# Pooled attention and channel mix on one core: x's first blocks ahead of the weights, a shorter float64 conversion, an earlier second block, two exponentials ahead of squares

## The chip, the cores and the metric

The kernel runs on one core of one Trainium2 chip. The number that counts is the device time of one execution, in microseconds, from a launch to its end. The profile of one execution gives a span (first to last instruction); the execution's own time is a little longer than its span.

The engines are named as the profile names them: PE (matrix products; PEld is its weight load), DVE (vector), ACT (scalar functions), POOL (GpSimd) and SP, whose queue issues nearly all transfers here.

## What is computed

For each of B = 4 batches with N = 12608 tokens of 128 features, 32 inducing rows attend to all tokens, all tokens attend to the 32 results, and the outcome goes through an RWKV channel mix of inner width 1024.

```
def mab(q, kv):
    s = scale * (q @ kv.transpose(0, 2, 1))
    s = s - s.max(-1, keepdims=True)
    a = np.exp(s)
    a /= a.sum(-1, keepdims=True) + 1e-09
    return a @ kv
h = mab(I, x)          # I: the 32 inducing rows, for every batch
x = mab(x, h)
x_prev = np.concatenate([zeros, x[:, :-1, :]], axis=1)
xk = mu_k * x + (1.0 - mu_k) * x_prev
xr = mu_r * x + (1.0 - mu_r) * x_prev
k = np.maximum(xk @ w_k, 0.0)
v = k * k @ w_v
r = 1.0 / (1.0 + np.exp(-(xr @ w_r)))
return r * v
```

x, mu and the output are float32; the three weight matrices come as float64, so the kernel has to make float32 of them from their bit patterns.

## The kernel before

**Tiling.** A batch is six blocks of 2048 tokens and a tail of 320. A block is four groups of 512 tokens. Each group is four *units* of the channel mix; unit n does `up` (six matmuls into the two-bank tile `ps_a`), `square` (DVE takes the ReLU `k_t` at line 802, ACT squares it into the high part `kh` at line 807 and once more in full at line 808, POOL subtracts to the low part `kl` at line 810), and four steps later `down` (six matmuls into `ps_v`). There are 400 units, and the main loop runs over them by the step number n; two units' `up` stand together at even n. In steps 8, 12, 20, 24 and so on DVE makes `kh` itself (line 804).

**What else hangs on the steps.** Work beside the units is put into the loop by step: `at(n, f)` places f at the end of step n, `soon(n, f)` places it in step n ahead of that step's squares. `stage_a(b, j)` pools block j of batch b (the inducing rows' side) one batch ahead; `stage_b(b, j)` lets a block's tokens attend to the pooled rows, and spreads the result over the tiles `R` of its four groups by transfers.

**The head.** Batch 0 has nobody to run ahead of it, so `head()` pools its seven pieces in the order tail, block 0, ... block 5, indexed k = 0..6 there. For piece k: `tr` transposes x on PE and ACT copies it to `xt`; `scores` multiplies with the inducing rows; `maxi` takes the running maximum on DVE (lines 257 to 261); `expo` is on ACT (lines 272, 273); `etrans` (PE) and `ecopy` (DVE, line 285) turn the exponentials; `hmm` (PE, line 297) and `acc` (DVE, line 308) accumulate; `sums` (DVE, line 290) keeps the running sum. Between these, `place(n)` takes the next n steps off the list of weight conversions. The table `PARTS` says how many are taken where.

**A conversion** (`load_weight`, lines 85 to 135) of 128 x 512 weights takes six steps: exponent, mantissa, clamp, sign, low, power. DVE does lines 105, 109, 115, 120, 123, 127; ACT does 116 (mantissa to float) and 110 (ReLU of the exponent); POOL multiplies the parts at line 133. Five pieces are converted: two of w_k, two of w_v and a quarter-size one, w_r. `split_wv` (lines 159 to 164) then splits w_v into `wvh` and `wvl`.

**The loads.** The raw weights go to buffers `k_t` (w_r's to `oT`), blocks 0 to 3 of x to buffers `kh` and `kl` (two transfers of 512 KB per block, line 193), blocks 4 and 5 to the two `xb` buffers (eight of 256 KB, line 212), the tail to `xl`. Later batches load a block by one transfer of 1 MB into `xb` (line 207). All are issued by SP in program order.

**The end of the head and the start.** After piece 6's `etrans`, `spin(2)` runs ten matmuls on PE with no result that is used; then `weights_sum`, `hmm` and `hfin` give the pooled rows `hT`. `start()` makes the first four groups of stage B straight from x (`stage_b_first(g)`: `diff`, `expo` at line 725, `norm`, `turn` at line 744, `high` at 749, `low` at 753), partly ahead of the loop and partly in its first steps. Block 1 of batch 0 then goes through `stage_b` with `direct=True`; its exponential is at line 638.

**Next batch's blocks.** `stage_a(1, j)` transposes its block with four calls of `btr(c)` (DVE, line 344, into one of three `xs` buffers; then four transfers to `xt` at line 347). For block 0 these stand in steps 8 to 11, for block 1 in steps 15, 16, 17 and 19. The load of the block behind it is put at step t + 8, where t is the step at which the stage starts: for block 1 of batch 1 that is step 12.

Of the kernel before, what the change touches and what calls it, by code (L numbers as in the profile page):

```python
# [8 lines left out]
F32 = mybir.dt.float32  # L9
# [10 lines left out]
def kernel(  # L20
# [64 lines left out]
    def load_weight(dst, src, n, raw):  # L85
# [11 lines left out]
        def steps():  # L97
# [10 lines left out]
            def clamp():  # L108
                v.tensor_scalar(out=X.t, in0=X.t, scalar1=1151.0, scalar2=-896.0, op0=ALU.min, op1=ALU.add)
                nc.scalar.activation(out=X.t, in_=X.t, func=AF.Relu)  # L110
# [7 lines left out]
            def sign():  # L118
                X.r = st.tile([P, G], I32, name="aT")[:, :n]
                v.tensor_scalar(out=X.r, in0=hi, scalar1=-2147483648, scalar2=None, op0=ALU.bitwise_and)  # L120

# [4 lines left out]
            def power():  # L126
                v.scalar_tensor_tensor(out=X.t, in0=X.t, scalar=23, in1=X.r,
                                       op0=ALU.logical_shift_left, op1=ALU.bitwise_or)
                qv, tv = X.q, X.t.bitcast(F32)
                if len(dst.shape) == 3:  # L130
                    qv = qv.rearrange("p (c d) -> p c d", d=C)
                    tv = tv.rearrange("p (c d) -> p c d", d=C)
                nc.gpsimd.tensor_tensor(out=dst, in0=qv, in1=tv, op=ALU.mult)
            return [exponent, mantissa, clamp, sign, low, power]
# [191 lines left out]
    def stage_a(b, j, at, t):  # L326
# [151 lines left out]
        for bn, jn in order_a[k + 1:]:  # L478
            if jn < NBLK - 1:
                at(t + 8, lambda: load_x(bn, jn))  # L480
                if jn == NBLK - 2:
                    at(t + 8, lambda: load_x(bn, jt))
                break
# [119 lines left out]
    def stage_b(b, j, at, t, bank="b", direct=False, offsets=(0, 1, 1, 2, 3, 5, 5, 6, 6, 7, 9)):  # L603
# [80 lines left out]
        for n, f in zip(offsets, (scores, trans, maxi, sub, expo, total, recip, mult, back, high, low)):  # L684
            at(t + n, f)
# [196 lines left out]
    for j in order_h:  # L882
        load_x(0, j, pairs if j < 4 else None)
        if wloads:
            wloads.pop(0)()
# [12 lines left out]
    def spin(n):  # L898

        half = P // 2  # L900
        ps = pa.tile([P, 2, G], F32, name="ps_a")
        rhs = wvh.rearrange("p c d -> p (c d)")[:, :G]
        for i in range(3):
            nc.tensor.matmul(out=ps[:, i % 2, :], lhsT=wvh[:, i, :], rhs=rhs, start=True, stop=True)
        for i in range(n):
            for r in range(2):
                rows = slice(half * r, half * (r + 1))
                nc.tensor.matmul(out=ps[:, r, :], lhsT=wvh[rows, (i + r) % FC, :], rhs=rhs[rows],
                                 start=True, stop=True)
        for i in range(3):  # L910
            nc.tensor.matmul(out=ps[:, i % 2, :], lhsT=wvh[:, i, :], rhs=rhs, start=True, stop=True)


    PARTS_FIRST = 6
    PARTS = ((0, 0, 0), (3, 3, 0), (3, 3, 0), (3, 3, 0), (3, 3, 1), (1, 0, 0), (0, 0, 0))

    def head():
# [3 lines left out]
        for k in range(2):  # L921
            ab[k].tr()
        place(PARTS_FIRST)
        ab[0].scores()
        for k in range(NBLK):
# [7 lines left out]
            if k > 0:  # L933
                ab[k - 1].acc()
            if k == 0:
                constants()
            if k + 2 < NBLK:
                ab[k + 2].tr()
            place(PARTS[k][1])
# [3 lines left out]
            ab[k].etrans()  # L943
            ab[k].ecopy()
            if k < last:
                ab[k].sums()
                ab[k + 1].scores()
            place(PARTS[k][2])
        spin(2)
        weights_sum()  # L950
        ab[last].hmm()
# [14 lines left out]
    def start():  # L966
# [8 lines left out]
        plan = ((None, None, None, at, soon, soon, at), (at,) * 4 + (soon, soon, at), (at,) * 4 + (soon, soon, at))  # L975
# [15 lines left out]
    for b in range(B):  # L991
        t = b * UB + (4 if b == 0 else 0)
        for j in range(NBLK - 1):
# [6 lines left out]
            else:  # L1000
                stage_b(b, j + 1, at, 3, direct=True, offsets=(0, 1, 1, 1, 3, 4, 4, 4, 5, 6, 7))
# [75 lines left out]
```

## Time and profile before

| | us |
|---|---|
| runs, not profiled | 1123.52, 1127.31, 2022.45 |
| median of these | 1127.31 |
| the profiled execution's own time | 1123.31 |
| its span | 1121.5 |

The profile and the trace are of the execution that took 1123.31 us, of which 1121.5 us are the span and 1.8 us lie around it. A stretch is read from a view of busy time by windows, and a wait from a view in order of time: a row gives the start, the length, the engine, the line, the operation, the tiles, and in brackets how long the engine had been idle before it and what released it. A row of several instructions (x4) has the time of all of them. The mean granted clock of PE is 0.99 over the whole span.

### The profile page before, as it was taken

The page shows a single profiled execution, that of the slowest core. Times are in us where ns is not written, and L with a number is a line of the kernel's source. Part 1 is how long each engine was busy: PE and PEld are TensorE (multiplying, and loading weights), DVE is VectorE, ACT ScalarE, POOL GpSimd, SP SyncE. Part 2 cuts the span into 40 slices and gives each one's busy share as a digit, 9 for nine tenths or more (in the row PEclk, how much of TensorE's full clock was granted, in tenths as well). Part 3 has the DMA queues.
Part 4 walks back from the last instruction along what each step waited for, and adds up shares of the span by engine and source line. Part 5 has one row for each costly group of instructions (what it writes and reads, how often), then busy time and mean ns, then how long its engine had stood idle before and what let it go on. Part 6 is the DMA issues. An engine that isn't in the chain of part 4 may idle for free.

```text
span 1121.5 us, 19356 instructions
## 1 busy us (share of the span) xinstructions
PE 1077.1 (96%) x6610; PEld 736.2 (66%) x6610; DVE 913.1 (81%) x1301; ACT 962.4 (86%) x1101; POOL 948.3 (85%) x421
## 2 busy tenths in 40 slices
PE   5779899999999999999999999999999999999997
PEld 4546566666676666666766666667667666667775
DVE  5677789998678999998777899998776788888665
ACT  5486688898998988898998898999899989999995
POOL 2157599888888999888888998889889899999996
PEclk9999899999999999999999999999999999999998
DMA  9204575675327656757317646765414424453422
GB/s 274 77 1 119 115 155 135 146 175 133 60 39 164 138 133 144 169 134 158 60 29 139 156 109 154 162 157 114 86 31 94 91 48 95 87 97 71 88 38 35
DMA packets 267634, 123.61 MB, mean 110 GB/s; under 512 B 225648, under 2 KB 247056, under 8 KB 265232
## 3 DMA queue, kind: packets, MB, share of 16 engines
q1 hardware_dynamic: 267200, 122.35, 50.7%
q8 instruction: 53, 0.87, 0.3%
q14 instruction: 45, 0.37, 0.1%
q10 hardware_dynamic: 336, 0.02, 0.0%
HBM read 28.07 MB, written 25.82 MB: 48 GB/s over the span
## 4 chain that ended last, share of the span: by engine, by line
PE 84%; DVE 6%; SPq 4%; ACT 3%; issue 1%; DMA 1%; POOL 1%; DVEq 0%; ACTq 0%
PE ps_v L821 48%; PE ps_a L792 26%; PE ps_v L780 4%; DVE k_t L802 2%; PE pb_b L621 2%; PE pb_a L441 2%; PE pb_a L372 2%; DMA xb<-in_x_dram 1%; SPq L95 1%; ACT kh L807 1%; SPq L193 1%; SPq L601 1%; ACT k_t L808 1%; POOL kl L810 1%; DVE kh L804 1%
## 5 line engine op out<-in xcount | busy, mean ns | idle before, releaser
L810 POOL TENSOR_TENSOR kl<-k_t,kh 128x1024 fp32r<-128x1024 f32 (+2 forms) x400 | 936.6, 2381 | 135.9 <-ACT k_t L808 124.9
L802 DVE TENSOR_SCALAR k_t<-ps_a 128x1024 f32<-128x1024 f32 (+1 forms) x400 | 476.8, 1198 | 86.3 <-PE ps_a L792 64.4
L808 ACT ACTIVATE k_t<-k_t 128x1024 f32<-128x1024 f32 (+1 forms) x400 | 418.0, 1048 | 50.3 <-DVE kh L804 16.9
L807 ACT ACTIVATE kh<-k_t 128x1024 fp32r<-128x1024 f32 (+1 forms) x352 | 365.3, 1038 | 67.2 <-DVE k_t L802 66.7
L792 PE MATMUL ps_a<-R,W 64*128 64x512 f32 (+1 forms) x2400 | 332.1, 408 | 8.8 <-DVE k_t L802 7.0
L792 PEld LDWEIGHTS ps_a<-R,W 64*128 64x128 f32 x2400 | 209.4, 186 | 131.1 <-issue 52.4
L821 PE MATMUL ps_v<-kh,wvh 128*128 128x512 f32 (+1 forms) x800 | 272.3, 422 | 0.0
L821 PE MATMUL ps_v<-kl,wvh 128*128 128x512 f32 (+1 forms) x800 | 249.8, 393 | 1.7 <-POOL kl L810 1.2
L821 PE MATMUL ps_v<-kh,wvl 128*128 128x512 f32 (+1 forms) x800 | 249.9, 394 | 0.0
L821 PEld LDWEIGHTS ps_v<-kh,wvh 128*128 128x128 f32 x800 | 132.7, 189 | 95.2 <-issue 38.5
L821 PEld LDWEIGHTS ps_v<-kl,wvh 128*128 128x128 f32 x800 | 150.4, 189 | 37.6 <-POOL kl L810 2.2
L821 PEld LDWEIGHTS ps_v<-kh,wvl 128*128 128x128 f32 x800 | 150.3, 189 | 33.7
L826 DVE TENSOR_TENSOR oT<-ps_v,rT 128x512 f32<-128x512 f32 (+1 forms) x100 | 66.9, 669 | 25.0 <-PE ps_v L821 24.8
L780 PE MATMUL ps_v<-R,Wg 128*128 128x512 f32 (+1 forms) x200 | 64.2, 402 | 6.4 <-DVE oT L826 6.4
L837 DVE STREAM_TRANSPOSE ot<-oT 128x512 f32<-128x512 f32 x96 | 67.0, 698 | 0.0
L804 DVE SCALAR_TENSOR_TENSOR kh<-ps_a,k_t 128x1024 fp32r<-128x1024 f32 x48 | 58.8, 1225 | 1.7
L782 ACT ACTIVATE rT<-ps_v 128x512 f32<-128x512 f32 (+1 forms) x100 | 57.9, 579 | 0.3
L344 DVE STREAM_TRANSPOSE xs<-xb 128x512 f32<-128x512 f32 x72 | 49.9, 693 | 10.0 <-DMA xb<-in_x_dram 5.5
L780 PEld LDWEIGHTS ps_v<-R,Wg 128*128 128x128 f32 x200 | 37.2, 192 | 17.2 <-DVE oT L826 8.5
L782 ACT ACT_TABLE_LOAD x31 | 39.8, 1283 | 0.5
L667 DVE TENSOR_TENSOR hl<-pb_b,hl 128x512 fp32r<-128x512 f32 x23 | 15.9, 690 | 14.2 <-ACT hl L664 13.9
L621 PE MATMUL pb_b<-xt,hT 128*32 128x512 f32 x184 | 24.4, 603 | 0.6 <-DVE R L753 0.6
(217 smaller groups left out, 528.7 us busy)
## 6 DMA issues: line engine op xcount, KB each, us to landing
out_dram<-ot SPq DMA_DIRECT2D x184, 128.0 KB, 3.3
R<-R SPq DMA_DIRECT2D x88, 256.0 KB, 3.2
xb<-in_x_dram SPq DMA_DIRECT2D x18, 1024.0 KB, 5.8
xt<-xs SPq DMA_DIRECT2D x288, 64.0 KB, 2.0
R<-hl SPq DMA_DIRECT2D x96, 128.0 KB, 2.4
R<-hl SPq DMA_DIRECT2D x96, 127.8 KB, 2.4
kh<-in_x_dram SPq DMA_DIRECT2D x4, 512.0 KB, 7.9
kl<-in_x_dram SPq DMA_DIRECT2D x4, 512.0 KB, 7.5
```

The lines of the kernel that those rows point to most:

```text
L344: nc.vector.transpose(out=xs.rearrange("p (s q) -> p s q", q=M), in_=S.xb[j][:, :, M * c:M * (c + 1)])
L780: nc.tensor.matmul(out=ps[:, :w], lhsT=S.Wg, rhs=R[:, s, :w], start=(s == 0), stop=(s == 1))
L782: nc.scalar.activation(out=self.rT, in_=ps[:, :w], func=AF.Sigmoid)
L792: nc.tensor.matmul(out=ps[:, r, :w], lhsT=S.W[a][rows, u * P:(u + 1) * P], rhs=R[rows, k, :w], start=(n == 0), stop=(n == 2))
L802: nc.vector.tensor_scalar(out=k, in0=ps, scalar1=0.0, scalar2=None, op0=ALU.max)
L804: nc.vector.scalar_tensor_tensor(out=kh, in0=ps, scalar=0.0, in1=k, op0=ALU.max, op1=ALU.mult)
L807: nc.scalar.activation(out=kh, in_=k, func=AF.Square)
L808: nc.scalar.activation(out=k, in_=k, func=AF.Square)
L810: return lambda eng, a, z: eng.tensor_tensor(out=kl[:, :, a:z], in0=k[:, :, a:z], in1=kh.bitcast(F32)[:, :, a:z], op=ALU.subtract)
L821: nc.tensor.matmul(out=self.v, lhsT=wt[:, fc, :], rhs=kk[:, c, :], start=(fc == 0 and n == 0), stop=(fc == FC - 1 and n == 2))
L826: nc.vector.tensor_tensor(out=self.oT, in0=self.v, in1=self.rT, op=ALU.mult)
L837: nc.vector.transpose(out=ot[:, o:o + w], in_=self.oT)
```

## The change

Seven edits, in the order of the program:

1. `load_weight`: the step `sign` goes; `power` takes the sign bit and joins the exponent in one operation, since ACT's ReLU now scales by 2^23 and so does the shift; the order is exponent, clamp, mantissa, low, power. On ACT the ReLU thereby comes ahead of the mantissa.
2. The loads: the weights' five transfers are issued behind blocks 1, 2, 3, 4 and 5 of x, no longer behind the tail and blocks 0 to 3. They follow one another as before.
3. `head()`: the conversions start one piece later (no more `PARTS_FIRST`), in the rounds k = 1 to 5, and both `split_wv` come in round 5. `place(PARTS[k][1])` moves between `etrans` and `ecopy`. `sums` of a piece moves behind `acc` of that piece, one round later.
4. `warm(8)`: eight 128 x 128 matmuls of the identity, behind the tail's transposes.
5. `spin(3)`: three matmuls in place of ten, behind `weights_sum`.
6. `stage_a`: block 1 of batch 1 is loaded at step 2, not at step 12.
7. The exponentials of group 3 (line 725) and of block 1 (line 638) of batch 0 are put with `soon`, ahead of their step's squares.

```
             def clamp():
                 v.tensor_scalar(out=X.t, in0=X.t, scalar1=1151.0, scalar2=-896.0, op0=ALU.min, op1=ALU.add)
-                nc.scalar.activation(out=X.t, in_=X.t, func=AF.Relu)
+                nc.scalar.activation(out=X.t, in_=X.t, func=AF.Relu, scale=2.0 ** 23)
...
-            def sign():
-                X.r = st.tile([P, G], I32, name="aT")[:, :n]
-                v.tensor_scalar(out=X.r, in0=hi, scalar1=-2147483648, scalar2=None, op0=ALU.bitwise_and)
...
             def power():
-                v.scalar_tensor_tensor(out=X.t, in0=X.t, scalar=23, in1=X.r,
-                                       op0=ALU.logical_shift_left, op1=ALU.bitwise_or)
+                v.scalar_tensor_tensor(out=X.t, in0=hi, scalar=-2147483648, in1=X.t,
+                                       op0=ALU.bitwise_and, op1=ALU.bitwise_or)
...
-            return [exponent, mantissa, clamp, sign, low, power]
+            return [exponent, clamp, mantissa, low, power]
...
             if jn < NBLK - 1:
-                at(t + 8, lambda: load_x(bn, jn))
+                at(2 if (b, j) == (1, 0) else t + 8, lambda: load_x(bn, jn))
...
         for n, f in zip(offsets, (scores, trans, maxi, sub, expo, total, recip, mult, back, high, low)):
-            at(t + n, f)
+            (early if early and f is expo else at)(t + n, f)
...
         load_x(0, j, pairs if j < 4 else None)
-        if wloads:
+        if 0 < j < NBLK - 1:
             wloads.pop(0)()
...
+    def warm(n):
+
+        ps = pa.tile([P, 2, G], F32, name="ps_a")
+        for i in range(n):
+            nc.tensor.matmul(out=ps[:, i % 2, :P], lhsT=ident, rhs=ident, start=True, stop=True)
...
-    PARTS_FIRST = 6
-    PARTS = ((0, 0, 0), (3, 3, 0), (3, 3, 0), (3, 3, 0), (3, 3, 1), (1, 0, 0), (0, 0, 0))
+    PARTS = ((0, 0), (3, 2), (3, 2), (3, 2), (3, 2), (5, 2), (0, 0))
...
-        for k in range(2):
-            ab[k].tr()
-        place(PARTS_FIRST)
+        ab[0].tr()
+        warm(8)
+        ab[1].tr()
         ab[0].scores()
...
             if k > 0:
                 ab[k - 1].acc()
+                ab[k - 1].sums()
...
-            place(PARTS[k][1])
             if k == last:
                 ab[k].sums()
                 weights()
             ab[k].etrans()
+            place(PARTS[k][1])
             ab[k].ecopy()
             if k < last:
-                ab[k].sums()
                 ab[k + 1].scores()
-            place(PARTS[k][2])
-        spin(2)
         weights_sum()
+        spin(3)
         ab[last].hmm()
...
-        plan = ((None, None, None, at, soon, soon, at), (at,) * 4 + (soon, soon, at), (at,) * 4 + (soon, soon, at))
+        plan = ((None, None, None, at, soon, soon, at), (at,) * 4 + (soon, soon, at), (at, at, soon, at, soon, soon, at))
...
-                stage_b(b, j + 1, at, 3, direct=True, offsets=(0, 1, 1, 1, 3, 4, 4, 4, 5, 6, 7))
+                stage_b(b, j + 1, at, 3, direct=True, early=soon, offsets=(0, 1, 1, 1, 3, 4, 4, 4, 5, 6, 7))
```

Where the instructions stand now. In these lists a row is a line of the program, an operation, output<-inputs and a size; `x4` is four in a row. The changed program is a little shorter, so its line numbers in these rows are 4 smaller.

**SP, from its first transfer on.** The `k_t` and `oT` rows are the weights; `xl`, `kh`, `kl` and `xb` 128x4x128 are batch 0's x; `xb` 128x2048 is a block of batch 1. Before:

```order
L201 DMA xl<-in_x_dram 80x4x128
L95 DMA k_t<-in_moe_w_k_dram 128x1024
L193 DMA kh<-in_x_dram 128x8x128 x2
L95 DMA k_t<-in_moe_w_k_dram 128x1024
L193 DMA kh<-in_x_dram 128x8x128 x2
L95 DMA k_t<-in_moe_w_v_dram 128x4x256
L193 DMA kl<-in_x_dram 128x8x128 x2
L95 DMA k_t<-in_moe_w_v_dram 128x4x256
L193 DMA kl<-in_x_dram 128x8x128 x2
L95 DMA oT<-in_moe_w_r_dram 128x256
L212 DMA xb<-in_x_dram 128x4x128 x8
```

On the same engine, now:

```order
L197 DMA xl<-in_x_dram 80x4x128
L189 DMA kh<-in_x_dram 128x8x128 x4
L95 DMA k_t<-in_moe_w_k_dram 128x1024
L189 DMA kl<-in_x_dram 128x8x128 x2
L95 DMA k_t<-in_moe_w_k_dram 128x1024
L189 DMA kl<-in_x_dram 128x8x128 x2
L95 DMA k_t<-in_moe_w_v_dram 128x4x256
L208 DMA xb<-in_x_dram 128x4x128 x4
L95 DMA k_t<-in_moe_w_v_dram 128x4x256
L208 DMA xb<-in_x_dram 128x4x128 x4
L95 DMA oT<-in_moe_w_r_dram 128x256
```

Blocks 0 and 1 (`kh`) have no piece of the weights ahead of them now, where one and two stood; block 2 has one and block 3 two, where three and four stood; block 4 has three and block 5 four, where all five stood. w_r's small piece is behind them all.

**SP, the next rows**, up to the first spread of stage B's result (`R`). Before:

```order
L207 DMA xb<-in_x_dram 128x2048
L347 DMA xt<-xs 32x512 x16
L588 DMA R<-R 32x2x1 x2
L601 DMA R<-hl 32x1024
L601 DMA R<-hl 32x2x511
L601 DMA R<-hl 32x1024
L601 DMA R<-hl 32x2x511
L207 DMA xb<-in_x_dram 128x2048
L588 DMA R<-hl 32x2x1 x2
```

On the same engine, now:

```order
L203 DMA xb<-in_x_dram 128x2048 x2
L343 DMA xt<-xs 32x512 x16
L584 DMA R<-R 32x2x1 x2
L597 DMA R<-hl 32x1024
L597 DMA R<-hl 32x2x511
L597 DMA R<-hl 32x1024
L597 DMA R<-hl 32x2x511
L584 DMA R<-hl 32x2x1 x2
```

The load of block 1 of batch 1 is moved ahead of sixteen `xt` and six `R` transfers, and stands right behind block 0's.

**ACT, steps 5 to 7 of the loop** (`s_923` and `s_917` are the tile of line 638's exponential, `aT` that of group 3; the first ACT_TABLE_LOAD is for the exponential, the second for the sigmoid `rT`). Before:

```order
L807 ACTIVATE kh<-k_t 128x1024
L808 ACTIVATE k_t<-k_t 128x1024
L807 ACTIVATE kh<-k_t 128x1024
L808 ACTIVATE k_t<-k_t 128x1024
L638 ACT_TABLE_LOAD
L638 ACTIVATE s_923<-s_923 128x512
L725 ACTIVATE aT<-aT 128x256
L782 ACT_TABLE_LOAD
L782 ACTIVATE rT<-ps_v 128x512
```

On the same engine, now:

```order
L803 ACTIVATE kh<-k_t 128x1024
L804 ACTIVATE k_t<-k_t 128x1024
L634 ACT_TABLE_LOAD
L634 ACTIVATE s_917<-s_917 128x512
L721 ACTIVATE aT<-aT 128x256
L803 ACTIVATE kh<-k_t 128x1024
L804 ACTIVATE k_t<-k_t 128x1024
L778 ACT_TABLE_LOAD
L778 ACTIVATE rT<-ps_v 128x512
```

Step 6's two squares now stand between the exponentials and the sigmoid's table load; the number of table loads is the same.

More of the change, by code (lines that the diff above doesn't have):

```diff
@@ L601, in fill, with stage_b @@
             nc.sync.dma_start(out=rf[M * s:M * (s + 1), :, o + s % 2:o + s % 2 + m], in_=src[:, :, :m])
-    def stage_b(b, j, at, t, bank="b", direct=False, offsets=(0, 1, 1, 2, 3, 5, 5, 6, 6, 7, 9)):
+    def stage_b(b, j, at, t, bank="b", direct=False, early=None, offsets=(0, 1, 1, 2, 3, 5, 5, 6, 6, 7, 9)):
         S = batches[b]
@@ L898, in spin @@
     def spin(n):
-        half = P // 2
         ps = pa.tile([P, 2, G], F32, name="ps_a")
         rhs = wvh.rearrange("p c d -> p (c d)")[:, :G]
-        for i in range(3):
+        for i in range(n):
             nc.tensor.matmul(out=ps[:, i % 2, :], lhsT=wvh[:, i, :], rhs=rhs, start=True, stop=True)
+    def warm(n):
+        ps = pa.tile([P, 2, G], F32, name="ps_a")
         for i in range(n):
[L906 to L911, printed above, removed]
-    PARTS_FIRST = 6
-    PARTS = ((0, 0, 0), (3, 3, 0), (3, 3, 0), (3, 3, 0), (3, 3, 1), (1, 0, 0), (0, 0, 0))
+            nc.tensor.matmul(out=ps[:, i % 2, :P], lhsT=ident, rhs=ident, start=True, stop=True)
+    PARTS = ((0, 0), (3, 2), (3, 2), (3, 2), (3, 2), (5, 2), (0, 0))
     def head():
         last = NBLK - 1
-        for k in range(2):
-            ab[k].tr()
-        place(PARTS_FIRST)
+        ab[0].tr()
+        warm(8)
+        ab[1].tr()
         ab[0].scores()
```

## The prediction

> **What bounds the kernel now.** I read the engines' totals first, then busy time by stage, then the first 140 us in order of time, engine by engine, and last SP's queue beside them.
>
> ```profile
> PE 1077.1 (96%) x6610; PEld 736.2 (66%) x6610; DVE 913.1 (81%) x1301; ACT 962.4 (86%) x1101; POOL 948.3 (85%) x421
> ```
>
> ```profile
> core 0: us, PE busy (x) PEld busy (x) DVE busy (x) ACT busy (x) POOL busy (x), PEclk, DMA share, GB/s
> 0.00:136.00 136.00, 105.89 (x865) 69.73 (x869) 95.67 (x192) 83.28 (x127) 62.33 (x43) 0.94 0.46 116
> 44.00:60.00 16.00, 12.19 (x150) 7.45 (x150) 10.48 (x31) 3.49 (x7) 0.00 (x0) 1.00 0.15 60
> 60.00:64.00 4.00, 3.20 (x22) 2.25 (x22) 3.46 (x6) 3.13 (x5) 3.37 (x2) 0.62 0.00 0
> 136.00:1121.50 985.50, 971.24 (x5753) 666.51 (x5745) 817.43 (x1110) 879.08 (x975) 885.93 (x379) 1.00 0.52 109
> ```
>
> From 136 us on PE is busy for 971.2 of 985.5 us at full clock, and no edit touches an instruction there. So the change can only move the first 136 us, and what it saves there moves the end by as much. PE's whole idle time before 136 us is 136 - 105.9 = 30.1 us. A 2% change, which is about what a measurement of this kernel can tell from none, is 22.5 us: three quarters of all that idle time would have to go.
>
> **The head: the loads (edits 2 and 4).**
>
> ```profile
> 8.80 3.71 PE L230 MATMUL ps_a<-ident,kh 128*128 128x128 f32 x16 [4.47 <-DMA kh<-in_x_dram]
> ...
> 15.47 1.06 PE L230 MATMUL ps_a<-ident,kh 128*128 128x128 f32 x8 [0.71 <-DMA kh<-in_x_dram]
> ...
> 34.04 1.97 PE L230 MATMUL ps_a<-ident,xb 128*128 128x128 f32 x16
> ```
>
> ```profile
> 17.91 0.69 DVE L257 TENSOR_REDUCE mx<-ps_v 128x1 f32<-128x512 f32 x1 [0.53 <-PE ps_v L252]
> ...
> 28.41 0.68 DVE L257 TENSOR_REDUCE mx<-ps_v 128x1 f32<-128x512 f32 x1
> ...
> 33.70 0.68 DVE L257 TENSOR_REDUCE mx<-ps_v 128x1 f32<-128x512 f32 x1
> ...
> 41.58 0.68 DVE L257 TENSOR_REDUCE mx<-ps_v 128x1 f32<-128x512 f32 x1
> ```
>
> PE waits for block 0's first half until 8.80 and for block 1's second half until 15.47. In SP's order 1.21 and 3.31 MB are queued up to the ends of these two (0.16 MB for the tail, 0.52 for each 512 KB transfer), so data lands at 6.67 us / 2.10 MB = 3.18 us per MB. Now block 1's second half stands at 2.26 MB: by the same line it lands at 8.80 + 1.05 x 3.18 = 12.1 us, 3.3 earlier. The maximum at 17.91, round 1's, hangs on it through PE (transposes, a small transposition, scores), so it comes 3.3 earlier too.
>
> `warm` has PE's idle 4.47 us ahead of it; I cost it at nothing. If block 0 landed at once it would stand in the way by at most 8 x 0.23 (3.71 / 16 a matmul) = 1.9 us, and the wait for block 1 would still hide that.
>
> What is late next are the weights, since a DVE wait for them would hold up everything behind it, `ecopy` and the next maximum first. The first piece now ends at 2.78 MB, 13.8 us, and is wanted after round 1's maximum, at 15.6; the last large one ends at 7.50 MB, 28.8 us, and is wanted near 31. So no wait, with 2 us to spare.
>
> The loads as a whole gain nothing: the bytes are the same. Their last, 8.68 MB, lands at 32.5 us by that line, and the last x only w_r's 0.13 MB sooner, where block 5 is used from 34.04 on: there it can come at most some 2 us earlier than now.
>
> **The head: conversions and sums (edits 1 and 3).**
>
> ```profile
> 29.31 0.15 DVE L261 TENSOR_SCALAR nb<-mx 128x1 f32<-128x1 f32 x1
> ...
> 31.08 0.69 DVE L123 SCALAR_TENSOR_TENSOR e1t<-k_t,e1t 128x512 f32<-128x512 uint32 x1
> 31.69 0.68 DVE L127 SCALAR_TENSOR_TENSOR s<-s,aT 128x512 int32<-128x512 int32 x1
> 32.30 0.68 DVE L285 COPY e<-pb_b 128x512 f32<-128x512 f32 x1
> 32.90 0.88 DVE L290 SCALAR_TENSOR_TENSOR sum<-sum,alpha,ss 128x1 f32<-128x1 f32 x1
> ```
>
> ```profile
> 30.94 0.62 ACT L110 ACTIVATE s<-s 128x512 int32<-128x512 int32 x1
> ...
> 39.62 0.61 ACT L162 CAST wvh<-ot 128x512 fp32r<-128x512 f32 x1
> ```
>
> ```profile
> 32.45 1.30 POOL L133 TENSOR_TENSOR ot<-e1t,s 128x512 f32<-128x512 f32 x1 [3.99 <-DVE s L127]
> ```
>
> A round with a large conversion takes 33.70 - 28.41 = 5.29 us now, and DVE hardly stops in it. Without `sign` it is not shorter by that step: `low` (L123) waits for the mantissa from ACT, which now comes second there. Counted from 29.39, when the next instruction follows `nb`: ACT's second conversion step ends at 31.56, so `low` starts at 2.2 instead of 1.7; `low`, `power` and `ecopy` take 0.61 each from start to start, which is 4.0; from a maximum's start to there is 1.0 (29.39 - 28.41). A round is 5.0 us. `sums`, 0.88 long here behind `ecopy`, goes into DVE's new wait for ACT and costs nothing there. That is 0.25 less in each of three rounds, 0.7 in all. But round 4 had the quarter-size conversion, and rounds 4 and 5 took 41.58 - 33.70 = 7.9; now round 4 has a large one and round 5 the small one: 5.0 + 4.0 = 9.0, 1.1 more. For x that lands late in rounds 2 and 3 (blocks 3 and 4, by the line above at 22.2 and 27.1) I add 0.2. The maximum at 41.58 thus comes 3.3 + 0.7 - 1.1 - 0.2 = 2.7 earlier.
>
> Both `split_wv` now stand in round 5, which has no transposes for ACT to copy; while it waits for the last maximum there is room for two casts of 0.61. Uncovered they would cost 1.2.
>
> Why the old `sums` took so long decides a part of this: it ends at 33.78, and POOL's product at 33.75. The Trainium skill ("SBUF — State Buffer", section "Who interferes with whom") says that a DVE instruction with two SBUF inputs and a GpSimd one that reads SBUF lock each other out for a whole instruction. The trace agrees here. By that rule the new place, with no POOL product beside it, is free; were the 0.88 the instruction's own time, a round would still be 5.0, since the wait for ACT is 0.9 long.
>
> **The end of the head (edit 5).**
>
> ```profile
> 44.49 0.94 PE L904 MATMUL ps_a<-wvh 128*128 128x512 f32 x3
> ...
> 46.84 0.28 PE L519 MATMUL pb_b<-ws,stack 128*128 128x1 f32 x2
> 47.04 1.08 PE L297 MATMUL pb_a<-xb,e 128*32 128x128 f32 x32
> ```
>
> ```profile
> 44.77 0.69 DVE L285 COPY e<-pb_a 128x512 f32<-128x512 f32 x1 [0.42 <-PE pb_a L280]
> ```
>
> `hmm` (47.04) needs only DVE's copy, done at 45.46; the ten matmuls hold it up. Now L519 (0.28) and three matmuls (0.94) start at 44.5, so `hmm` starts at 45.7, 1.3 earlier. The head gains 2.7 + 1.3 = 4.0 us; its bounds are 1.3 (the spin alone) and 3.3 + 0.7 + 1.3 = 5.3.
>
> **The exponentials (edit 7).**
>
> ```profile
> 74.44 1.06 ACT L808 ACTIVATE k_t<-k_t 128x1024 f32<-128x1024 f32 x1
> ...
> 78.81 1.28 ACT L638 ACT_TABLE_LOAD   x1
> ```
>
> ```profile
> 75.32 2.35 DVE L802 TENSOR_SCALAR k_t<-ps_a 128x1024 f32<-128x1024 f32 x2 [0.90 <-PE ps_a L792]
> 80.77 0.69 DVE L642 TENSOR_REDUCE pb_b<-s 128x16 f32<-128x512 f32 x1 [3.10 <-ACT s L638]
> ```
>
> DVE waits 3.10 us for line 638, 80.77 - 78.81 = 1.96 after its table load began. Now that load starts when the square of 74.44 ends, at 75.5, and the result is there at 77.5, before DVE is done with 75.32 + 2.35 = 77.67: the wait is gone, and PE, which waited for DVE in turn, is served sooner. Step 6's squares move behind, some 1.2 us later than now; what waits for them is POOL's `kl`, wanted by PE four steps on. I take 3.0 (bounds: 1.5 if that lateness reaches PE, and 3.1).
>
> **The second block (edit 6).**
>
> ```profile
> 103.53 0.58 SPq L207 DMA_DIRECT2D xb<-in_x_dram  x1
> 104.22 2.06 SPq L588 DMA_DIRECT2D R<-hl  x2
> ...
> 121.60 10.05 SPq L347 DMA_DIRECT2D xt<-xs  x16
> ```
>
> ```profile
> 111.04 0.71 DVE L344 STREAM_TRANSPOSE xs<-xb 128x512 f32<-128x512 f32 x1 [5.50 <-DMA xb<-in_x_dram]
> ...
> 125.69 0.71 DVE L344 STREAM_TRANSPOSE xs<-xb 128x512 f32<-128x512 f32 x1 [4.14 <-DMA xt<-xs]
> ```
>
> ```profile
> SPq L844 <- DMA xb<-in_x_dram: 1.5, 1, 1.5
> ```
>
> The load moves past sixteen `xt` and six `R` transfers on SP, to a place where SP has nothing else to issue and the transfer engines are empty (share 0.00 in 60 to 64); it only has to wait for block 5's `hmm` to free the buffer. So it is there long before step 15, and DVE's wait of 5.50 us is gone. DVE's second wait, 4.14 us, is for an `xs` buffer, whose transfers SP reaches only at 121.60, behind all `R` transfers of block 1 and four of the output. That wait grows, because DVE is there sooner and SP is not as much sooner. SP loses the load's issue (0.7 from 103.53 to 104.22), the 1.5 that an output transfer waited for that load, and what its neighbours were slowed beside its traffic: two small issues took 2.06 us where SP's usual pace is near 0.6 each, so 0.8 here and some 0.4 elsewhere. That is 3.4 us, with bounds of 2.2 (the first two alone) and 9.6 (both DVE waits). The second wait is then 4.14 + 5.50 - 3.4 = 6.2 us.
>
> **The sum.** 4.0 + 3.0 + 3.4 = 10.4 us off the profiled execution's 1123.3: **1112.9 us**. That execution lies 4.0 under the median of the runs shown and 0.2 under the lowest; the range has to hold a run that is 4 higher.
>
> **The rivals.**
> - *Both DVE waits go.* If SP caught up, 9.6 in place of 3.4: 1106.7 us. For it: PE alone would then set the pace. Against: SP issues a transfer in 0.63 us at best (10.05 / 16 in the row at 121.60), and 28 of them stand ahead of the `xt` ones.
> - *The head gains only the spin.* If the extra large conversion eats the early x, 10.4 - 2.7 = 7.7 off: 1115.6 us. For it: the loads end when they did. Against: block 5 was used 1.5 us after the end of all loads.
> - *The clock.* Two rows of PE on it:
>
> ```profile
> 58.43 0.96 PE L792 MATMUL ps_a<-R,W 64*128 64x512 f32 x6 [0.41 <-DVE k_t L802]
> 60.80 1.50 PE L792 MATMUL ps_a<-R,W 64*128 64x512 f32 x6 [1.41 <-DVE k_t L802]
> ```
>
> The granted clock fell at 60 us (0.62 in 60 to 64), and the same six matmuls took 1.50 us for 0.96. Seven matmuls fewer before 47 may bring such a fall forward. One stretch of 4 us costs about 2 (PE's 3.20 busy us less 0.62 of them, and its followers), two cost 4: 1115 to 1117 us.
> - *Slower than before*, by that mechanism alone: at half clock from 44 to 60 PE's 12.2 busy us double. It decides once more than 10.4 of them lie on the path; with all of them 1123.3 - 10.4 + 12.2 = 1125.1 us. Against: PE is idle for a quarter of that time, waiting for others.
>
> The Trainium skill ("TensorE: Matmul & The Clock Gate", Part 1) lets the clock fall after an idle window of about 3.4 us. By that rule the new head, with no idle time of that length behind its loads, loses nothing, and the time stays at 1112.9. The trace does not bear the length out: the idle time at the fall at 60 us was 1.41.
>
> **Chances.** The sum's case 0.60, with a range of its own of 1109 to 1117; both waits gone 0.10; spin only 0.15; the clock 0.09; slower than before 0.04; none of these 0.02. The range 1107 to 1120 leaves out most of the first rival, the slower one and the last. All cases but a sliver lie within 2%: faster 0.03, same 0.94, slower 0.03.
>
> **What would show it.** Right: block 1's second half used near 12 us; rounds of 5.0 us; `hmm` right behind three matmuls; no wait of line 642's reader; none for `xb`, and 5 to 7 us at the fourth transposition of block 1. Wrong: that last wait short; `low` not waiting for ACT; a clock under 1 between 40 and 56 us; a DVE wait for raw weights.

## The result, and the profile after

The changed kernel took 1118.57 us (median of six runs, 1114.72 to 1120.00) beside 1125.76 us for the kernel before on the same chip; the ratio is 0.9932, with a 95% interval of 0.991 to 0.9955. It is 5 to 10 us shorter: clear of the noise, but under the 2% that counts as a change here. One of the kernel before's six runs took 2022.45 us; without it their median is 1125.12. The forecast was 1112.9, 5.7 us lower: about 3 us of the 10.4 promised did not arrive, and 2.5 come from the base, since the forecast started from an execution of 1123.3 us and the median here is 1125.76. Measured again (e9), the same program gave 1116.02 us (five runs) against 1124.18, ratio 0.9927 [0.9914, 0.994].

The profiled execution took 1118.54 us, 1116.7 of them its span. First the engines' totals and busy time by windows (columns as in the prediction; the number ahead of "DMA share" is the granted clock of PE):

```profile
PE 1079.7 (97%) x6619; PEld 737.6 (66%) x6619; DVE 912.0 (82%) x1296; ACT 962.5 (86%) x1101; POOL 948.2 (85%) x421
```

```profile
0.00:136.00 136.00, 113.70 (x917) 75.11 (x918) 99.37 (x193) 89.23 (x134) 67.43 (x45) 0.94 0.51 129
40.00:42.00 2.00, 0.51 (x9) 0.23 (x9) 1.34 (x5) 1.09 (x4) 0.57 (x1) 0.88 0.42 94
42.00:44.00 2.00, 1.77 (x8) 1.70 (x9) 1.24 (x6) 0.16 (x1) 0.00 (x0) 0.50 0.97 406
...
48.00:50.00 2.00, 1.72 (x22) 1.00 (x25) 1.36 (x7) 0.00 (x0) 0.00 (x0) 0.50 0.79 266
50.00:52.00 2.00, 2.00 (x25) 0.94 (x18) 1.36 (x4) 0.89 (x2) 0.00 (x0) 0.56 0.54 225
```

PE is busy 7.8 us more of the first 136 us than before (113.7 for 105.9). That is work that has come forward, not a worse clock: the mean granted clock of the stretch is 0.94 in both. The clock is at half from about 41.5 to 51.8 us now, and again from 120.0 to 126.9; the kernel before has the same 17 us of half clock in four pieces, from 61, 84.9, 112.2 and 128.7 us. Then the head, DVE in order of time:

```profile
14.13 0.69 DVE L253 TENSOR_REDUCE mx<-ps_v 128x1 f32<-128x512 f32 x1 [0.74 <-PE ps_v L248]
...
21.75 0.21 DVE L286 SCALAR_TENSOR_TENSOR sum<-sum,alpha,ss 128x1 f32<-128x1 f32 x1
22.52 0.69 DVE L119 SCALAR_TENSOR_TENSOR e1t<-k_t,e1t 128x512 f32<-128x512 uint32 x1 [0.56 <-ACT e1t L116]
...
34.50 0.69 DVE L253 TENSOR_REDUCE mx<-ps_v 128x1 f32<-128x512 f32 x1
35.23 0.17 DVE L255 TENSOR_TENSOR mx<-mx,mx 128x1 f32<-128x1 f32 x1
...
38.65 0.67 DVE L253 TENSOR_REDUCE mx<-ps_v 128x1 f32<-128x512 f32 x1
39.36 1.23 DVE L255 TENSOR_TENSOR mx<-mx,mx 128x1 f32<-128x1 f32 x1
...
48.04 0.19 DVE L531 COPY hT<-pb_b 128x32 f32<-128x32 f32 x1 [0.73 <-PE pb_b L529]
```

Round 1's maximum starts at 14.13 for 17.91, the last at 38.65 for 41.58: 2.9 us earlier. But `hT`, the head's result, comes at 48.04, only 1.0 before the 49.04 of the kernel before (its row stands below). Behind the last maximum two things take time that was not there. Line 255, the running maximum of 128 x 1 numbers, takes 1.23 us where it took 0.16 or 0.17 in every earlier round and in the last one of the kernel before; the row of POOL shows what ran beside it:

```profile
38.07 2.50 POOL L159 TENSOR_TENSOR wvl<-ot,wvh 128x512 fp32r<-128x512 f32 x2
```

These are the two differences of `split_wv`, 1.25 us each, the second from 39.32 to 40.57; line 255 ends at 40.59. Before, the second of them ran from 40.37 to 41.65 us, and it was a `sums` that stood beside it and took 0.59 us (0.21 in the next round); line 259, as it was then, came behind it:

```profile
41.07 0.59 DVE L290 SCALAR_TENSOR_TENSOR sum<-sum,alpha,ss 128x1 f32<-128x1 f32 x1
...
42.30 0.16 DVE L259 TENSOR_TENSOR mx<-mx,mx 128x1 f32<-128x1 f32 x1
```

And PE's rows behind the changed kernel's line 255 are at half clock:

```profile
43.40 1.63 PE L899 MATMUL ps_a<-wvh 128*128 128x512 f32 x3
44.96 1.94 PE L293 MATMUL pb_a<-xb,e 128*32 128x128 f32 x32
```

The three matmuls of `spin` take 1.63 us where the prediction counted 0.94, `hmm` 1.94 for 1.08.

At the other end of the head, `warm` and the first block:

```profile
4.66 3.35 PE L905 MATMUL ps_a<-ident 128*128 128x128 f32 x16 [0.32 <-ACT xtl L231]
7.84 1.91 PE L226 MATMUL ps_a<-ident,kh 128*128 128x128 f32 x16
```

The eight matmuls of `warm` are sixteen instructions in the profile and take 3.35 us. Block 0's first half lands at 6.0 (issued at 1.18, 4.8 us to landing) and is used at 7.84; block 1's second half lands at 11.8 and is used at 11.89, so `warm` stood in the way of block 0 but not of round 1. Block 0's sixteen transposes take 1.91 us here for 3.71 before, although the granted clock reads 1.00 in both.

Last the two DVE waits further on, the queue of SP, and the place at which I compare executions from here on: line 437 (line 441 before), the next batch's `hmm` of block 1, behind which no edit moves anything.

```profile
75.92 0.68 DVE L638 TENSOR_REDUCE pb_b<-s 128x16 f32<-128x512 f32 x1
...
100.77 0.71 DVE L340 STREAM_TRANSPOSE xs<-xb 128x512 f32<-128x512 f32 x1
...
118.32 0.71 DVE L340 STREAM_TRANSPOSE xs<-xb 128x512 f32<-128x512 f32 x1 [7.92 <-DMA xt<-xs]
```

```profile
82.84 10.86 SPq L343 DMA_DIRECT2D xt<-xs  x16
...
114.23 10.06 SPq L343 DMA_DIRECT2D xt<-xs  x16
```

```profile
120.75 1.22 PE L776 MATMUL ps_v<-R,Wg 128*128 128x512 f32 x2 [5.96 <-DVE oT L822]
...
128.74 1.08 PE L437 MATMUL pb_a<-xb,e 128*32 128x128 f32 x32
```

And the head's result and line 441 of the kernel before:

```profile
49.04 0.19 DVE L535 COPY hT<-pb_b 128x32 f32<-128x32 f32 x1 [0.50 <-PE pb_b L533]
```

```profile
135.46 1.08 PE L441 MATMUL pb_a<-xb,e 128*32 128x128 f32 x32
```

Line 638's reader waits no more, nor does block 1's first transposition, at 100.77, wait for `xb`; the wait at the fourth transposition grew from 4.14 to 7.92, and PE stands idle for 5.96 us behind it. By line 437 the gain is 6.7 us. What follows it took 1116.7 - 128.74 = 988.0 us, against 1121.5 - 135.46 = 986.0 before: among others PE's clock fell at a batch boundary near 350 us in this execution (0.87 and 0.79 granted in 345 to 355 us) and did not there in the one before (1.00). Over all fourteen profiled executions this rest is 985.9 to 990.4 us, so a time of one execution tells kernels apart only to some 3 or 4 us, and the rows before 136 us have to say the rest.

### The profile page after: what moved, and what is told of

Its sections match the earlier page's. It is cut to its first block, busy times and chain, and to the rows that moved or that the text cites. A ratio compares the mean times of both kernels' runs of the same rounds, so it can differ in the third digit from the quotient of the medians.

```text
span 1116.7 us, 19364 instructions
## 1 busy us (share of the span) xinstructions
PE 1079.7 (97%) x6619; PEld 737.6 (66%) x6619; DVE 912.0 (82%) x1296; ACT 962.5 (86%) x1101; POOL 948.2 (85%) x421
## 4 chain that ended last, share of the span: by engine, by line
PE 87%; DVE 5%; ACT 3%; SPq 2%; issue 1%; DMA 1%; POOL 0%; DVEq 0%; ACTq 0%
PE ps_v L817 50%; PE ps_a L788 26%; PE ps_v L776 4%; PE pb_b L617 2%; DVE k_t L798 2%; PE pb_a L368 2%; PE pb_a L437 2%; ACT kh L803 1%; SPq L189 1%; SPq L95 1%; ACT k_t L804 1%; DMA xb<-in_x_dram 1%; DVE kh L800 0%; POOL kl L806 0%; PE pb_a L552 0%
```

## The experiments

All are the changed kernel with one thing altered, but for e4, which leaves out two edits, and e8, e11 and e12, which combine; e9 alters nothing. Edit 4, `warm`, has no run of its own. The table has, in us, the start of the last maximum, line 255 there, the start of `hT`, how long PE's clock was at half between 36 and 68 us (worked out from two-us windows as the missing clock x 2 / 0.5, and where it begins), the start of line 437, the median, and the ratio to the kernel before, measured beside it.

| | last max. | L255 | `hT` | half clock, from | L437 | median | ratio |
|---|---|---|---|---|---|---|---|
| before | 41.58 | 0.16 | 49.04 | 3.4, 61 | 135.46 | | |
| changed | 38.65 | 1.23 | 48.04 | 10.2, 41.5 | 128.74 | 1118.57 | 0.9932 [0.991, 0.9955] |
| e9 changed again | 38.53 | 1.23 | 47.38 | 3.4, 43.1 | 127.26 | 1116.02 | 0.9927 [0.9914, 0.994] |
| e1 scalar maximum | 39.31 | 0.21 | 45.75 | none | 125.83 | 1116.44 | 0.9929 [0.9907, 0.9952] |
| e2 ten matmuls | 38.67 | 1.22 | 49.03 | 3.4, 42.5 | 128.26 | 1117.97 | 0.9946 [0.9928, 0.9964] |
| e3 four `xs` | 39.41 | 1.23 | 48.07 | 3.4, 44.3; 3.4, 55 | 120.43 | 1112.54 | 0.99 [0.9878, 0.9922] |
| e4 head only | 39.03 | 1.22 | 48.38 | 10.2, 43.2 | 134.29 | 1122.81 | 0.9977 [0.9958, 0.9997] |
| e5 no early load | 39.52 | 1.22 | 46.89 | 3.4, 59 | 129.42 | 1119.76 | 0.9952 [0.9939, 0.9964] |
| e6 no early exp. | 39.54 | 1.22 | 48.20 | 3.4, 44.4; 3.4, 55 | 130.87 | 1120.65 | 0.9961 [0.9947, 0.9976] |
| e7 old load order | 43.55 | 1.23 | 50.94 | 3.4, 63 | 131.44 | 1120.57 | 0.9967 [0.9955, 0.9979] |
| e8 e1 and e3 | 39.50 | 0.21 | 45.96 | none | 118.36 | 1110.36 | 0.9871 [0.9853, 0.989] |
| e10 mantissa first | 38.60 | 1.22 | 47.96 | 10.2, 42.8 | 128.76 | 1116.72 | 0.9932 [0.9914, 0.9949] |
| e11 e3 without early load | 39.12 | 1.22 | 47.57 | 6.8, 44.5 | 123.17 | 1114.26 | 0.991 [0.9893, 0.9927] |
| e12 e1, e3 and e10 | 38.66 | 0.21 | 45.10 | none | 117.44 | 1109.21 | 0.9875 [0.9851, 0.9899] |

**e1: the running maximum with one tensor input.**

```diff
-nc.vector.tensor_tensor(out=L.mx, in0=L.mx, in1=S.mrun, op=ALU.max)
+nc.vector.tensor_scalar(out=L.mx, in0=L.mx, scalar1=S.mrun, scalar2=None, op0=ALU.max)
```

> One edit to the changed kernel: the running maximum of the head takes the old maximum as a per-partition scalar (tensor_scalar) and not as a second tensor. Theory A (POOL's split of w_v locks out the two-input maximum of round 6 for 1.1 us, and the longer idle time of PE there lets the clock fall at 41.7 us): that maximum takes 0.2 us for 1.23, the clock stays at 1.00 through 46 us, hmm starts near 42.5 for 44.96, and the time is 3 to 4 us below the changed kernel's 1118.6, near 1115. Rival B (the clock falls because seven matmuls of the spin are missing): the maximum is 1.1 us earlier, the clock still falls between 40 and 52 us, and the time is near 1117.5.

```profile
40.02 0.21 DVE L255 TENSOR_SCALAR mx<-mx,mx 128x1 f32<-128x1 f32 x1
```

POOL's differences run beside it as before, and it takes 0.21 us: the 1.23 was a hold. From the last maximum to `hT` it is now 6.44 us; with the hold and at full clock (e5) 7.37. So the hold costs 0.93 us on the path. The clock did not fall between 36 and 68 us in this execution, and line 437 is 2.9 us earlier than in the changed kernel, 1.4 than in e9. The time does not tell it from the changed kernel: the ratios are 0.9929 and 0.9932. So the hold is shown, theory A's 3 to 4 us are not.

**e2: ten matmuls in the new place.** `spin(10)` for `spin(3)`.

> One edit to the changed kernel: ten matmuls in the spin for three, at the new place. Rival B (the missing matmuls let the clock fall): it does not fall before 52 us, or is back by 48, and the time is 1 to 2 us below 1118.6. Theory A: the fall comes at 41.7 us, before the spin starts, so it comes anyway; seven more matmuls at half clock cost 7 x 0.45 = 3 us on the path to hmm, which starts near 48 for 44.96, and the time is 1 to 3 us higher.

The clock fell at 42.5 all the same, and was back 3.4 us later for 10.2. Neither theory holds whole: the missing matmuls are not what brings the fall; whether they let it last is not shown either, since e9, with three, has 3.4 too. Beside e9, whose fall was as long, `hT` lies 10.36 us behind the last maximum for 8.85. The ten matmuls take 3.71 us for 1.55 of the three, mostly at half clock, and `hmm`, which then comes behind the fall, 1.08 for 1.93: 1.5 us more in all, half of theory A's 3.

**e3: four buffers for `xs`.** In all three places that name it:

```diff
-xs = st.tile([P, G], F32, name="xs", bufs=3)
+xs = st.tile([P, G], F32, name="xs", bufs=4)
```

> One edit to the changed kernel: four xs buffers for three, so that the fourth transposition of block 1 of batch 1 waits for no transfer. Theory A (DVE, and behind it PE, wait there only for the buffer, and nothing else needs those transfers soon): the wait of 7.92 us goes, PE's idle 5.96 us goes with it and the half clock behind it too, and the time falls by 6 to 8 us, to about 1111. Rival B (the late transfers to xt are wanted anyway): a wait of several us appears at the scores of that block (line 368) or at its maximum, and less than 2 us are gained.

```profile
109.91 0.70 DVE L340 STREAM_TRANSPOSE xs<-xb 128x512 f32<-128x512 f32 x1
...
136.27 0.71 DVE L340 STREAM_TRANSPOSE xs<-xb 128x512 f32<-128x512 f32 x1 [2.54 <-DMA R<-hl]
```

The fourth transposition waits for nothing, line 437 is 8.3 us earlier, and 2.54 come back as a wait for another transfer. As theory A had it, PE's idle 5.96 us goes too, and the half clock of 6.8 us with it: the granted clock is 1.00 from 58 to 160 us. The time falls by 3.6 us in the ratios (0.9932 to 0.99, intervals that overlap) and by 6 in the medians (3.5 beside e9's), less than the 6 to 8 expected. The wait for an `xs` buffer was on the path, and it was what the second block's edit had left over.

**e4: the head alone.** The changed kernel without edits 6 and 7.

> The head's edits alone (1 to 5), with the second block's load and the two exponentials as before. Theory A (the head gives 2.9 us at the last maximum and loses most of it to the lock and the clock): the first step's ReLU comes 0.5 to 1.7 us earlier than before, the waits of 3.1, 5.5 and 4.1 us are there as before, and the time is 0.5 to 2 us below the kernel before. Rival B (the head's early x carries through): 4 us below.

2.6 us by the ratio (0.3 to 4.7), with the hold, and a clock at half for 10.2 us in the profiled execution, whose first ReLU (line 798) is even 0.3 us later than before (57.48 for 57.16) and whose line 437 is 1.2 us earlier. Nearer to theory A, though its ReLU did not come earlier; the interval does not exclude B's 4 us. The waits are there: 3.10 for line 638, 3.87 for `xb` and 5.93 at the fourth transposition, the last two 9.80 together for 9.64 before.

**e5: without edit 6, and e6: without edit 7.**

```diff
-at(2 if (b, j) == (1, 0) else t + 8, lambda: load_x(bn, jn))
+at(t + 8, lambda: load_x(bn, jn))
```

> The changed kernel without edit 6 (block 1 of the next batch is loaded where it was before). Theory A (the early load is worth only what SP loses by it, 2.5 us, since the fourth transposition waits for SP either way): the wait for `xb` at the third transposition is back at 4 to 6 us, the wait at the fourth falls from 7.9 to 3.5 to 6 us, their sum rises by about 2.5, and the time is about 2.5 above the changed kernel's 1118.6, 1120 to 1122 us. Theory B (the whole wait for `xb` was gained): the wait at the fourth transposition stays at 7 to 8 us beside 4 to 6 for `xb`, and the time is 1123 us or more. Theory C (the load's place only moves the wait): the sum of both waits stays at 7.9 and the time at 1118.6.

e5's two waits, at block 1's first transposition (the expectation calls it the third) and at its fourth:

```profile
103.95 0.71 DVE L340 STREAM_TRANSPOSE xs<-xb 128x512 f32<-128x512 f32 x1 [3.83 <-DMA xb<-in_x_dram]
...
119.27 0.71 DVE L340 STREAM_TRANSPOSE xs<-xb 128x512 f32<-128x512 f32 x1 [5.60 <-DMA xt<-xs]
```

Their sum is 9.43, for 7.92 in the changed kernel and 7.83 in e9. From one block's first `xt` issue to the next's SP takes 115.17 - 82.19 = 32.98 us, against 114.23 - 82.84 = 31.39 with edit 6 and 33.98 before. So edit 6 by itself is worth 1.5 to 1.6 us in the rows (2.3 by the ratios, with intervals that overlap): theory A's mechanism with less than its 2.5. The whole 3.83 (B) it is not; C is the farther from the rows, but the times alone would not exclude it. Of SP's waits, the output transfer's for the load is 0.5 us here, where it was 1.5 before:

```profile
SPq L840 <- DMA xb<-in_x_dram: 0.5, 1, 0.5
```

> The changed kernel without edit 7 (exponentials behind the squares, as before). Theory A (the 3.1 us wait lies on the path of PE to the end): DVE waits 3.0 to 3.2 us for line 638, everything behind it is 3 us later, and the time is 1121 to 1122.5 us. Theory B (SP's queue, not DVE, sets the fourth transposition, and SP does not hang on this step): the wait of 3.1 is back, but the wait at the fourth transposition is shorter by 2 to 3 us, and the time stays within 1 us of 1118.6.

```profile
78.82 0.69 DVE L638 TENSOR_REDUCE pb_b<-s 128x16 f32<-128x512 f32 x1 [3.10 <-ACT s L634]
```

The wait is back to a hundredth, the one at the fourth transposition stays at 7.81, and that transposition starts 2.8 us later than in the changed kernel. The ratio says 3.3 us (0.9961 for 0.9932, intervals that overlap). Theory A holds, not B. With the wait comes more than the wait: PE stands idle for 3.04 us until 82.03, and its clock is at half for 3.4 us from 82.0. Before it was the same, and with edit 7 there is neither:

```profile
83.98 1.15 PE L744 MATMUL pb_a<-ident,aT 128*64 128x128 f32 x16 [3.02 <-DVE aT L734]
```

**e7: the loads in the old order**, all else changed.

```diff
-if 0 < j < NBLK - 1:
+if wloads:
```

> The changed kernel without edit 2 (weights queued ahead of the first blocks of x, as before). Theory A (round 1 hangs on block 1's second half): PE waits for it until 14 to 15.5 us again, the maximum of round 1 starts at 17 to 18 us for 14.1, the last one 2 to 3.5 later than 38.65, and the time is 1120 to 1122 us. Theory B (the loads end when they did and later blocks bind): the maxima of rounds 1 and 2 are 3 us later, that of the last round by less than 1 us, and the time stays within 1 us of 1118.6.

Theory A, and more than it expected: round 1's maximum is at 19.48, later even than the 17.91 of the kernel before, and the last one is 4.9 us later than in the changed kernel. A part of that is the clock, which fell in this execution at 15.4 us for 3.4 us (0.84, 0.50 and 0.81 granted in the windows from 14 to 20):

```profile
15.89 1.94 PE L226 MATMUL ps_a<-ident,kh 128*128 128x128 f32 x8 [0.68 <-ACT xt L231]
```

Block 1's last eight transposes start 0.4 us later than before (15.47) and take 1.94 us for 1.06, the scores behind them 1.43 for 1.06; so some 1.2 us of the lateness are the clock's. Whether the old order brings this fall or only this execution had it, one profile does not show. The fourth transposition is 3.4 later, the ratio says 4 us (intervals that touch). The new conversion and its places need the new load order.

**e8: e1 and e3 together.**

> The changed kernel with the running maximum of line 255 as an operation with one tensor input and a scalar per partition, and with four buffers for `xs`. Theory A (the two costs, the lock at line 255 with the clock's fall behind it and the wait for an `xs` buffer, lie one behind the other on the path): line 255 takes 0.2 us, no wait at the fourth transposition, and the time is 2 us under that of four buffers alone (1112.5): 1109.5 to 1111.5 us. Theory B (the clock falls somewhere anyway, so the first repair is worth only its own 1 us or nothing): 1111.5 to 1113.5 us, with a granted clock under 1 somewhere between 42 and 60 us.

```profile
40.00:42.00 2.00, 1.15 (x37) 0.68 (x27) 1.23 (x7) 1.18 (x4) 1.42 (x2) 1.00 0.21 33
42.00:44.00 2.00, 1.76 (x13) 1.16 (x14) 1.63 (x8) 0.08 (x1) 0.00 (x0) 1.00 0.80 324
```

1110.36 us, 12 to 17 us under the kernel before: theory A in its range, though the intervals of e8 and e3 overlap. The granted clock is 1.00 in every window up to 160 us. Line 437 is 2.1 us before e3's. Of the 7.5 us that it is before e1's, 3.08 come back at 134.73, as a wait for a transfer to `R`.

**e9: the changed kernel once more.**

> The changed kernel as it is, in another profiled execution. Theory A (the clock's fall at 41.7 us belongs to an execution, not to the program): the conversions, line 255 at 1.2 us and the waits of 7.9 and 6.0 us come again to within 0.1 us, the fall does not, or at another place, and without it `hT` lies 7.3 to 7.4 us behind the last maximum instead of 9.4. Theory B (the changed head itself brings the fall): the granted clock is 0.5 from 42 to 50 us again. Time in both cases 1116 to 1120 us.

```profile
42.00:44.00 2.00, 1.80 (x9) 1.40 (x9) 1.63 (x7) 0.04 (x1) 0.00 (x0) 0.78 0.92 385
44.00:46.00 2.00, 2.00 (x30) 1.36 (x32) 0.07 (x1) 0.00 (x0) 0.00 (x0) 0.50 0.00 0
46.00:48.00 2.00, 1.25 (x30) 0.68 (x23) 0.97 (x6) 0.00 (x0) 0.00 (x0) 0.86 0.24 33
```

The hold (1.23) and the waits (7.83 at the fourth transposition) come again to 0.1 us; the fall comes later by 1.6 us and lasts 3.4 us, not 10.2. So where exactly it falls and for how long belongs to the execution (theory A, at another place). That the changed head makes a fall near there likely is not excluded: this execution was not free of it either.

**e10: the mantissa ahead of the clamp**, so that ACT makes first what `low` waits for.

```diff
-return [exponent, clamp, mantissa, low, power]
+return [exponent, mantissa, clamp, low, power]
```

> The changed kernel with the mantissa ahead of the clamp in the conversion, so that ScalarE makes first what `low` waits for. Theory A (DVE sets the rounds and stops only for ScalarE): `low` waits 0.1 us or not at all for 0.56 to 0.59, the large rounds take 4.4 to 4.6 us for 5.0 to 5.2, the last maximum starts at 36.5 to 37.2 us for 38.65, and the time is 1.5 to 2 us under the changed kernel's. Theory B (the rounds then wait for x or for PE): rounds of 4.8 us or more with a DVE wait for PE ahead of a maximum, the last one at 38 us or later, and no change of the time.

```profile
24.23 0.69 DVE L253 TENSOR_REDUCE mx<-ps_v 128x1 f32<-128x512 f32 x1 [0.33 <-PE ps_v L248]
...
29.76 0.69 DVE L253 TENSOR_REDUCE mx<-ps_v 128x1 f32<-128x512 f32 x1 [0.33 <-PE ps_v L248]
```

`low` waits 0 to 0.34 us in the large rounds, and in its place the maxima of rounds 2 to 5 wait 0.33 us for PE; the last one starts at 38.60. PE's transposes for their part wait for x, 0.50 us at 21.67 and 0.18 to 0.27 at 25.22, 26.86 and 31.82. Theory B: the wait for ACT was real and worth nothing here, since the rounds then stop for PE and for the arriving x. The time beside e9's says the same.

**e11: four `xs` buffers without edit 6.**

> Four buffers for `xs`, without edit 6 (block 1 of the next batch is loaded where it was before); to be set beside four buffers with edit 6, 1112.5 us. Theory A (edit 6 gained little because the wait for an `xs` buffer took back most of it): without that wait, the wait for `xb`, 3.5 to 4 us, lies whole on the path, and the time is 1115.5 to 1117 us. Theory B (SP or another engine absorbs it behind that place as well): 1113 to 1114 us, with the wait for `xb` there but PE back on the same time by 140 us.

Block 1's first transposition waits 2.90 us (the view puts it down to a transfer to `R`), and line 437 is 2.7 us later than in e3, so by the rows the wait lies whole on the path there. The time, 0.991 for 0.99, is within the intervals of no difference, and in the profiled execution the rest was 985.9 for e3's 988.5. Theory A at that place; what of it reaches the end stays open.

**e12: all three.**

> The changed kernel with all three: one tensor input at line 255, four buffers for `xs`, the mantissa ahead of the clamp. If the shorter rounds reach the path: 1.5 to 2 us under the 1110.4 of the first two, 1108 to 1109.5 us. If they do not: 1109.5 to 1111.5 us.

1109.21 us, in the range of the first case, but a ratio of 0.9875 for e8's 0.9871. In the profiled executions the last maximum is 0.84 us earlier than in e8 and line 437 0.92; with one and the same head the last maximum lies anywhere from 38.53 to 39.54. So nothing shows that the mantissa's place adds anything, as e10 said, and e8, the smaller edit, is the version to keep.

## Why the prediction was right, and where its terms were off

The range of 1107 to 1120 held the time, but only just. 1118.57 lies outside the 1109 to 1117 that the prediction gave its likeliest case (the 1116.02 of e9 lies inside); what held it is the room left for the rivals and for a run 4 us above the profiled one. The hold at line 255 was in none of these, so that the range covers it too is luck. What came is a gain of under 1% made up of the three parts forecast. The sum was about 3 us too good; by its steps:

- *Only the first 136 us move.* Held to within the scatter: 986.0 us behind line 437 before, 988.0 and 987.5 in the changed kernel's two executions, 985.9 to 990.4 in all.
- *Early x.* Forecast 3.3 for round 1, measured 3.8, and 2.7 to 3.8 over the twelve executions with this order (14.08 to 15.25 us); block 1's second half landed at 11.8 for 12.1 forecast. e7 shows that it is this edit. `warm` cost nothing, as forecast, but its bound of 1.9 us was too low: it took 3.35 us, and in some executions 3.8. Whether it gains anything no run shows.
- *Rounds of 5.0 us, `low` waiting for ACT, `sums` free.* 5.22, 4.98, 5.16, 5.01 and 4.15; the wait is 0.56 to 0.74, `sums` 0.21 (0.38 in the last round, where a POOL product ran beside it once more). The last maximum came 2.9 us earlier for 2.7 forecast; the other eleven executions with the new load order have 2.0 to 3.1. But the wait for ACT was only the last of two limits of about the same length (e10).
- *Both `split_wv` in round 5 cost nothing.* This step failed. It priced the two casts on ACT and left out the two differences on POOL, one of which now stands over the last round's line 255: 0.93 us on the path (e1 against e5). The rule quoted for `sums` named exactly this, two inputs from SBUF beside a POOL instruction that reads SBUF, and was applied to one instruction and not to the others in the moved step's neighbourhood. The second difference had held a `sums` before; with `sums` moved away, line 255 stands there.
- *`hmm` 1.3 earlier.* Mis-sized: without hold and fall, `hT` follows the last maximum by 6.44 us for 7.46 before, so 1.0.
- *The clock.* It was kept out of the sum as a rival of 0.09, and its sign, a clock under 1 between 40 and 56 us, came beside the sum's own. In the profiled execution `hT` lies 9.4 us behind the last maximum, 2.0 more than at full clock with the same hold (e5); the old fall at 61 us did not come, and PE's six matmuls there were quick again (0.97 us). The prediction took that fall for the only one; the 0.94 in its own row for 0 to 136 us holds four, two of them beside PE's waits of 3.02 us (until 83.98) and 3.74 us (until 113.72).
- *Exponentials 3.0.* The wait of 3.10 is gone and returns whole without the edit (e6): 2.8 by the rows, 3.3 by the ratio. That the half clock of 3.4 us behind PE's wait goes with it was not in the sum.
- *Second block: SP loses 3.4, the next wait grows to 6.2.* The mechanism was right, the size was not. From line 638's reduction to the fourth transposition it was 125.69 - 80.77 = 44.9 us before and 118.32 - 75.92 = 42.4 now: 2.5, and the wait grew to 7.9. Edit 6 is worth 1.6 of it beside edit 7 (e5) and 2.1 without: SP's two `xt` rows start 33.34 us apart in e4, which has neither, and 31.27 in e6, which has edit 6. The rest, 0.6 of SP's 33.98 before, is gone in e4 already, with the head's edits alone. Of its terms the issue's 0.7 stands; the output transfer's 1.5 is 0.7 in e4 and 0.5 in e5; and 0.4 is left in e5 for the slowed neighbours, where 1.2 were put.
- *The other rivals.* Both DVE waits did not go; e3 shows that one more buffer takes the second away; a faster SP was not tried. That the head would gain the spin alone is excluded by the last maximum, and nothing made the kernel slower.

With 2.9 + 1.0 - 0.9 for the head, 2.8 and 2.5, the rows give 8.3 us with the head at full clock; e9, with one short fall, has 135.46 - 127.26 = 8.2, and the first profiled execution, with three times that fall, 6.7. Of the 10.4 forecast, the hold took 0.9, `hmm` 0.3 and the second block 0.9; the rest of the shortfall is the clock's, as far as the rows show.

## What to carry to other kernels

A moved step is priced on every engine that it uses, and its instructions on POOL also by what DVE runs beside them; here a DVE instruction of 128 x 1 took 1.23 us, longer than the 0.69 of one of 128 x 512. Where a wait for one transfer is taken away and the next wait is for a buffer that the same queue empties, a buffer more can be worth more than the moved transfer (e3: 8 us at line 437 and 3.6 by the ratios, edit 6: 1.6 and 2.3). Where executions of one program scatter by more than the effect, compare them by rows at a fixed place behind the change, and the times only by their ratios. Where PE waits for microseconds, look at the clock behind the wait as well: with the wait gone, the half clock behind it was gone too (e3, and edit 7 in e6).

## What the runs showed of the hardware that was not expected

**A hold of a whole instruction, even on 128 x 1.** Line 255 has 128 x 1 numbers and took 1.22 or 1.23 us beside POOL's difference in all ten profiled executions of the new head in which it has two tensor inputs, and 0.21 in the three with a scalar for its second input. The Trainium skill ("SBUF — State Buffer", "Who interferes with whom") names two SBUF inputs as the condition; the runs bear it out, also in that one tensor input beside the same POOL instruction goes free.

**The clock falls in steps of 3.4 us.** In eleven executions with a fall between 36 and 68 us, the half clock lasted 3.4, 6.8 or 10.2 us, once, twice or three times the same length (the table). The Trainium skill ("TensorE: Matmul & The Clock Gate", Part 1) describes a free-running window of about 3.4 us, whose place under a program varies from run to run; the lengths agree, and so do e9 and the first execution, where one program fell at 43.1 and at 41.5. What the prediction took from that page, that PE must stand idle for a whole such length, does not agree with these falls: the longest idle time of PE shortly ahead of the first in the changed kernel is 0.96 us.

```profile
36.69 0.66 PE L276 MATMUL pb_b<-ident,rT 128*128 128x128 f32 x4 [0.96 <-ACT rT L269]
...
40.73 0.27 PE L489 MATMUL pb_b<-ident,mx 128*1 128x128 f32 x1 [0.87 <-DVE mx L255]
```

What these falls, and e7's at 15.4, have in common is that PE was busy for only 1.45 to 2.24 of the 3.41 us ahead of them. Low stretches of that kind occur without a fall too (1.48 of 3.4 at 49 us in e8, and in e3 1.83 of the 3.41 us that end just where the next, with 1.75, begins), so where the bound lies is not shown. All ten executions with the hold have a fall between 41 and 67 us, eight of them before 45; the three without it have none, and the kernel before, without it too, one at 61. That the hold brings the early fall, by one more low stretch, would fit this and stays open: three executions are few, and e1's time is not measurably better.

**Further on, the falls stand beside PE's long waits.** All ten kernels with three `xs` buffers have a fall, or two, between 100 and 136 us, of 3.4 or 6.8 us, each beside an idle time of PE of 2.06 to 6.18 us (5.96 in the changed kernel, whose fall of 6.8 us begins at 120.0). The wait for line 638's exponential, with PE idle for 3.02 to 3.04 us, has a fall of 3.4 us in each of the three kernels without edit 7 (before, e4, e6), and the eleven with it have none there. The four kernels with four buffers have no fall from 60 to 136 us, and no idle time of PE above 1.41 us. So idle times longer than 3.4 us stand beside a fall here, and so do some that are shorter.
